# Attention with transposes two slots behind their scores and an exponential that works in place

## The chip, the cores and the metric

The kernel runs on one core of a Trainium2 chip. The metric is the device time of one execution in microseconds (us). Five engines work side by side, each through its own list of instructions and in the order of that list: TensorE (PE) multiplies and transposes, VectorE (DVE), ScalarE (ACT) and GpSimd (POOL) do the elementwise work, and SyncE (SP) hands transfers to the DMA queue. Each waits with semaphores for what the others have to deliver. PE writes its results to PSUM banks; another engine has to copy a bank out before PE may write to it again.

## The reference

```python
scores = scale * np.matmul(q, k.transpose(0, 1, 3, 2))      # 4 batches, 8 heads, 576 x 576
scores = scores + bias.transpose(2, 0, 1)[None]             # bias from a small network over distances
scores = scores - np.max(scores, axis=-1, keepdims=True)
attn = np.exp(scores)
attn = attn / (np.sum(attn, axis=-1, keepdims=True) + 1e-09)
x = np.matmul(attn, v)                                      # then (2304 tokens, 512)
...
x = (g(x @ w_in)) @ w_out                                   # g: hardswish, 2048 wide
x = (sigmoid(x @ w_gate) * (x @ w_val)) @ w_out2            # 1536 wide
```

The change touches the attention alone.

## The kernel before, in words

**Stages.** First the bias of the scores is computed and written to DRAM in 18 transfers, through tiles called `p` (`bias_out`, L548 to L558). Then come attention, the first feed-forward layer (from L601 on) and the second one.

**Units and steps.** Attention runs over 16 units, each a pair of heads of one batch (`NU`). A unit has nine steps. Steps 0 to 7 are the four chunks of 128 query rows for both heads (step s is chunk s//2 of head s%2), each against all 576 keys. Step 8 takes the last 64 rows of both heads together.

**What a step does.** `scores` (L332) multiplies queries and keys on PE into one of two `s` banks (L341; eight matmuls, because queries and keys are split into a high and a low part). VectorE adds the bias, scales, and keeps each row's extreme value in one custom instruction (L345) that writes the tile `u`. `expo` (L359) has ScalarE take the exponential of `u` with the row's extreme as its bias; it writes the tile `p`, and the sums of the rows go to `sums` (L361). The transposes `trans` (L393; L399 on PE, or L407 for step 8) turn the probabilities so that keys lie on partitions; the copies out of the `tr` bank into `ptm` stand in `evac` (L389 on ScalarE, L391 on VectorE). After steps 1, 3, 5 and 8, `trans_rem` (L411, L414) turns the 64 remaining keys into `ptr`. `invert` (L364) takes reciprocals of the sums and spreads them along rows, and `turn_inv` (L374, L378) turns them into `inv`. The products with the values, `av` (L423; L431 for the groups of 128 keys, L434 for the rest), go to the one `av` bank, and `av_out` (L443) multiplies by `inv` on VectorE into the tokens.

**Input.** `load_qk` and `load_v` issue the transfers of a unit's queries, keys and values (L288, L290, L294). `prep` (L303) makes the high and low parts: L309 on ScalarE, L313 and L317 on GpSimd.

**Order.** `slot_of_two(i)` issues the work of steps 2i and 2i+1 in a row: scores and loads, the products that the table `AV` gives to the slot, the exponentials, `invert` of the slot before, `turn_inv` of two slots before, the transposes of the slot before (not ahead of the slot's last score matmul), then `prep`. There are `NSLOT` slots. A scheduler takes these instructions and settles the order of each engine; it may move them past one another where dependences allow. Around it the weight loader of the feed-forward layer is called every six slots (`load.whole`, L158 to L192), `split_x(0)` at slot 72, and the first two projections of the feed-forward layer ("early projections", `begun`) at slots 73 and 74, of which the ones on PE are L601 to L603 and the evictions L607 and L608.

**Buffers.** PSUM has two `s` tiles of two banks, three `tr` banks and one `av` bank. In SBUF `u` has three buffers, `p` three (each holds a chunk of both heads), `vn` two; `spread`, `inv`, `ptm`, `ptr` have one each.

Of the kernel before, what the change touches and what calls it, by code (L numbers as in the profile page):

```python
# [10 lines left out]
F32 = mybir.dt.float32  # L11
F32R = mybir.dt.float32r
I32 = mybir.dt.int32
AF = mybir.ActivationFunctionType
# [4 lines left out]
P = 128  # L19
B, H, S, D = 4, 8, 576, 64  # L20
# [5 lines left out]
NSTEP = 9  # L26
# [69 lines left out]
def block_kernel(ctx: ExitStack, tc: tile.TileContext, q, k, v, mlp, w_in, w_out, w_gate, w_val, w_out2, dist_d,  # L96
                 rows_d, out):
    nc = tc.nc
# [166 lines left out]
    a2 = attn.enter_context(tc.tile_pool(name="a2", bufs=2))  # L265
# [14 lines left out]
    low, sums = [stat[:, i] for i in range(2)], [stat[:, i] for i in range(2, 5)]  # L280
# [44 lines left out]
    NS = NU * NSTEP  # L325
    ptm = apool.tile([P, 2, 4, S], F32, name="ptm")
    ptr = apool.tile([P, S], F32, name="ptr")
    pts, us, avs, last_u, last_s = {}, {}, {}, [None], [None]
# [3 lines left out]
    def scores(t):  # L332
        n, s = seq[t]
        Q, K = Qs[n % 2], Ks[n % 2]
        ps = pp.tile([P, 2, 512], F32, name="s")
        todo = [(s % 2, s // 2)] if s < 8 else [(0, 4), (1, 4)]
        for a in range(2):
            mm = [(h, c, r) for h, c in todo for r in range(2)]
            for i, (h, c, r) in enumerate(mm):
                q0 = (0, S + P)[h] + P * c if c < 4 else (512, S)[h]  # L340
                last_s[0] = nc.tensor.matmul(ps[:, a, 0:HS], Q[:, q0 : q0 + P], K[:, r, h, HS * a : HS * a + HS],  # L341
                                 start=(i == 0), stop=(i == len(mm) - 1))
        u = a2.tile([P, S], F32, name="u", bufs=3)
        bt = bias_t[s // 2][:, s % 2] if s < 8 else bias_m
        last_u[0] = nc.vector.tensor_tensor_reduce(  # L345
            out=halves(u), in0=ps[:, :, 0:HS], in1=halves(bt), op0=ALU.add, op1=ALU.min, scale=-0.125, scalar=3e38,
            accum_out=low[n % 2][:, s : s + 1])
        us[t] = u

    def probs(t):  # L350
        n, s = seq[t]
        if s < 8:
            c, h = divmod(s, 2)
            if h == 0:
                pts[n, c] = a2.tile([P, 2, S], F32, name="p", bufs=3)
            return pts[n, c][:, h]
        return Pm[n % 2][:, 64:]

    def expo(t):  # L359
        n, s = seq[t]  # L360
        nc.scalar.activation(probs(t), us.pop(t), AF.Exp, bias=low[n % 2][:, s : s + 1], scale=-1.0,  # L361
                             accum_out=sums[n % 3][:, s : s + 1])

    def invert(n, c0, c1):  # L364
# [82 lines left out]
    REM = {1: 0, 3: 1, 5: 2, 8: 3}  # L447
    last_v = [None]

    NSLOT = NS // 2 + 4  # L450
    AV = {}
    for n in range(NU):
        i = (NSTEP * n + 5) // 2 + 2
        j = max(i + 2, (NSTEP * n + 8) // 2 + 2)
        for a, first in ((0, i), (1, j)):
            AV[first] = [(n, a, g) for g in range(3)]
            AV[first + 1] = [(n, a, g) for g in range(3, 5)]

    def steps(i):
        return [t for t in (2 * i, 2 * i + 1) if 0 <= t < NS]  # L460

    def slot_of_two(i):

        for t in steps(i):
            scores(t)
            n, s = seq[t]
            p, b = divmod(n, B)
            if s == 0:
                last_v[0] = load_v(n)
            if b == B - 1 and p + 1 < NPAIR and (s % 2 == 1 or s == 8):  # L470
                load_bias(p + 1, s // 2)
        for n, a, g in AV.get(i, ()):
            av(n, a, g)
            if g == 4:
                av_out(n, a)
        for t in steps(i):
            expo(t)
        for t in steps(i - 1):
            n, s = seq[t]
            if s in (5, 8):  # L480
                invert(n, s // 6 * 3, s // 6 * 2 + 3)
        for t in steps(i - 2):
            n, s = seq[t]
            if s in (5, 8):
                turn_inv(n, s // 6 * 3, s // 6 * 2 + 3)
        for t in steps(i - 1):
            n, s = seq[t]
            with tc.issue_after(last_s[0].ins):
                trans(t)
                if s in REM:  # L490
                    trans_rem(n, REM[s])
        for t in steps(i):
            if t in PREP:
                n, h = PREP[t]
                prep(n, h)
            for k, (n, h) in PREP.items():
                if h == 1 and n + 1 < NU and t == k + 3:
                    load_qk(n + 1)
# [6 lines left out]
    with ExitStack():  # L505
# [41 lines left out]

        def bias_out(G, ps):  # L548
            if G % 2 == 0:
                evs[0] = a2.tile([P, 2, S], F32, name="p", bufs=3)  # L550
            ev = evs[0]
            b = corr[:, 1:2] if G % ACT_SKIP == ACT_SKIP - 1 else corr[:, 0:1]
            nc.scalar.activation(halves(ev[:, G % 2]), ps[:, :, 0:HS], AF.Identity, bias=b, scale=rpsi8[:, G : G + 1])
            if G % 2 == 1:
                c, r = divmod(16 * (G - 1), P)
                last_b[0] = nc.sync.dma_start(nbias[c][r : r + 32].rearrange("(g i) h j -> (i h) g j", g=2), ev)
                if r == P - 32 or G == S // 16 - 1:
                    load_bias(0, c)  # L558

        evs, last_b = [None], [None]  # L560
# [175 lines left out]
        for part2, t in todo:  # L736
            for f in range(NH * part2, NH * part2 + NH):
# [9 lines left out]
                if part2 and t in (3, 5) and f % NH == NH - 3:  # L747
                    j = t // 4
# [168 lines left out]
```

## Time and profile before

| | |
|---|---|
| median of three runs | 1172.85 us (1172.06 to 1176.66) |
| profiled execution | 1173.17 us |
| its span, first to last instruction | 1171.4 us |
| mean granted clock of TensorE | 0.998 |
| busy: PE, weight loads, DVE, ACT, POOL | 98%, 87%, 66%, 50%, 35% |
| data moved by DMA | 236.87 MB, 202 GB/s in the mean |
| first scores; end of attention's stage | 60.60 us; about 349 us |

A busy PE has some matmul in flight. The ends of matmuls are modelled in the profile, so that 98% does not say that it runs at its peak. The weight loads (PEld) overlap the matmuls and have their own share. An engine's idle time is put down to the instruction that ended it. Start times count from the beginning of the span.

### The profile page before, as it was taken

How to read it: one execution, taken by the hardware profiler on the slowest of the kernel's cores; microseconds unless marked ns; L12 is line 12 of the kernel's file. 1: busy time of each engine (PE TensorE's matmuls, PEld its weight loads, DVE VectorE, ACT ScalarE, POOL GpSimd, SP SyncE). 2: the span in 40 equal slices, each digit the busy share in tenths (PEclk: the TensorE clock that was granted, in tenths of full speed). 3: DMA queues.
4: the chain of work that ended last, by engine and by line, in shares of the span. 5: the costliest groups of instructions: out<-in, count | busy, mean ns of one | idle time of the engine just before them, and what ended most of it. 6: DMA issues, size and time to landing. Idle time of an engine off the chain costs nothing.

```text
span 1171.4 us, 19580 instructions
## 1 busy us (share of the span) xinstructions
PE 1149.3 (98%) x7086; PEld 1020.6 (87%) x7086; DVE 772.2 (66%) x1484; ACT 590.0 (50%) x1272; POOL 413.9 (35%) x342
## 2 busy tenths in 40 slices
PE   8999999999999899999999999999999999999998
PEld 3467777777779899999999999999898998998997
DVE  8967787878868777447376576576357646543443
ACT  7978878787855455444454544443223222221211
POOL 0055445545305333233155534363223313311211
PEclk9999999999999999999999999999999999999999
DMA  6653635335213555339565658888768858757532
GB/s 205 252 150 96 209 92 183 100 103 165 95 43 120 189 206 193 131 120 320 216 243 215 250 183 333 340 319 326 273 232 279 319 172 321 280 179 263 189 109 72
DMA packets 80737, 236.87 MB, mean 202 GB/s; under 512 B 9088, under 2 KB 11904, under 8 KB 80640
## 3 DMA queue, kind: packets, MB, share of 16 engines
q1 hardware_dynamic: 80640, 235.62, 57.9%
q8 instruction: 56, 0.92, 0.3%
q14 instruction: 41, 0.34, 0.1%
HBM read 154.45 MB, written 81.13 MB: 201 GB/s over the span
## 4 chain that ended last, share of the span: by engine, by line
PE 78%; DVE 10%; ACT 4%; issue 4%; DMA 3%; POOL 1%; SPq 0%; DVEq 0%; POOLq 0%; ACTq 0%
PE o L664 12%; PE h L798 11%; PE o L798 11%; PE s L341 6%; PE o L853 6%; PE h L853 6%; PE av L431 5%; PE tr L399 4%; PE h L602 4%; PE h L601 4%; PE h L603 4%; PE s L575 2%; DVE z L185 2%; PE av L434 1%; DMA third<-in_part_dram 1%
## 5 line engine op out<-in xcount | busy, mean ns | idle before, releaser
L664 PE MATMUL o<-gh,slot 128*128 128x384 f32 x768 | 196.9, 337 | 6.4 <-ACT take L389 4.2
L664 PEld LDWEIGHTS o<-gh,slot 128*128 128x128 f32 x768 | 139.0, 189 | 8.7 <-ACT take L389 4.5
L664 PE MATMUL o<-gl,slot 128*128 128x384 f32 x384 | 129.4, 337 | 0.8 <-DVE gl L650 0.8
L361 ACT ACTIVATE p<-u,stat 128x576 f32<-128x576 f32 x128 | 98.7, 773 | 31.8 <-DVE stat L345 31.2
L341 PE MATMUL s<-k,q 128*128 128x288 f32 x640 | 112.2, 310 | 2.1 <-POOL k L317 1.0
L192 POOL TENSOR_TENSOR hl<-corners,hl 128x512 fp32r<-128x512 f32 x42 | 58.2, 1394 | 157.0 <-ACT hl L191 135.6
L650 DVE TENSOR_TENSOR gl<-g,gh 128x384 fp32r<-128x384 f32 x94 | 73.3, 779 | 60.2 <-ACT gh L649 60.0
L345 DVE CUSTOM_DVE_ANT_0 u<-s,bias 128x576 f32<-128x576 f32 x128 | 93.6, 753 | 26.7 <-PE s L341 26.2
L608 DVE SCALAR_TENSOR_TENSOR g<-g,h 128x384 f32<-128x384 f32 x94 | 51.7, 550 | 73.6 <-ACT g L607 73.4
L834 POOL TENSOR_TENSOR gp<-s,gp 128x384 fp32r<-128x384 f32 x36 | 39.7, 1115 | 160.0 <-PE h L798 104.3
L341 PEld LDWEIGHTS s<-k,q 128*128 128x128 f32 x640 | 89.1, 189 | 5.4 <-POOL k L313 1.9
L431 PE MATMUL av<-ptm,vn 128*64 128x288 f32 x512 | 78.2, 419 | 1.2 <-DVE x L443 0.7
L798 PE MATMUL o<-x,slot 128*128 128x384 f32 x432 | 77.8, 335 | 0.0
L798 PE MATMUL h<-x,slot 128*128 128x384 f32 x432 | 77.8, 335 | 0.0
L798 PEld LDWEIGHTS h<-x,slot 128*128 128x128 f32 x432 | 75.2, 188 | 0.7
L798 PEld LDWEIGHTS o<-x,slot 128*128 128x128 f32 x432 | 75.1, 188 | 0.0
L399 PE MATMUL tr<-ident,p 128*128 128x128 f32 x512 | 72.2, 275 | 2.2 <-ACT inv L389 1.5
L664 PEld LDWEIGHTS o<-gl,slot 128*128 128x128 f32 x384 | 72.5, 189 | 1.8 <-DVE gl L650 1.8
L649 ACT CAST gh<-g 128x384 fp32r<-128x384 f32 x94 | 48.1, 512 | 51.5 <-DVE g L608 51.0
L607 ACT ACTIVATE g<-h,half 128x384 f32<-128x384 f32 x94 | 54.2, 576 | 37.6 <-PE h L603 37.5
L317 POOL TENSOR_TENSOR q<-early,q 64x640 fp32r<-64x640 f32 (+1 forms) x30 | 44.2, 1485 | 74.3 <-ACT q L309 72.9
L834 POOL TENSOR_TENSOR x<-s,x 128x384 fp32r<-128x384 f32 x36 | 41.1, 1150 | 82.2 <-ACT x L833 48.1
(157 smaller groups left out, 2714.9 us busy)
## 6 DMA issues: line engine op xcount, KB each, us to landing
w<-hl SPq DMA_DIRECT2D x67, 512.0 KB, 3.4
slot<-w SPq DMA_DIRECT2D x67, 512.0 KB, 5.8
raw<-in_part_dram SPq DMA_DIRECT2D x50, 512.0 KB, 3.7
x<-xc SPq DMA_DIRECT2D x56, 384.0 KB, 6.2
sum<-sum SPq DMA_DIRECT2D x72, 256.0 KB, 3.1
early<-xc SPq DMA_DIRECT2D x28, 384.0 KB, 6.4
nbias<-p SPq DMA_DIRECT2D x18, 576.0 KB, 3.1
early<-in_part_dram SPq DMA_DIRECT2D x32, 288.0 KB, 4.4
```

The costliest lines, as they stand in the source:

```text
L192: eng.tensor_tensor(out=slot[:, 1], in0=z, in1=slot[:, 0].bitcast(F32), op=ALU.subtract)
L341: last_s[0] = nc.tensor.matmul(ps[:, a, 0:HS], Q[:, q0 : q0 + P], K[:, r, h, HS * a : HS * a + HS], start=(i == 0), stop=(i == len(mm) - 1))
L345: last_u[0] = nc.vector.tensor_tensor_reduce(out=halves(u), in0=ps[:, :, 0:HS], in1=halves(bt), op0=ALU.add, op1=ALU.min, scale=-0.125, sc ...
L361: nc.scalar.activation(probs(t), us.pop(t), AF.Exp, bias=low[n % 2][:, s : s + 1], scale=-1.0, accum_out=sums[n % 3][:, s : s + 1])
L399: nc.tensor.transpose(ps[:, kc], pts[n, c][:, h, 64 * h + P * kc : 64 * h + P * kc + P], ident)
L431: nc.tensor.matmul(ps[64 * h : 64 * h + 64, 0:HS], vt[:, 4 * h + g], ptm[:, h, g, cols], start=(g == 0), stop=False)
L607: nc.scalar.activation(g, ph, AF.Relu, bias=half, scale=1.0 / 6.0)
L650: last_g[0] = nc.vector.tensor_tensor(out=gl, in0=g, in1=gh.bitcast(F32), op=ALU.subtract)
L664: nc.tensor.matmul(os[c][:, 0:TW], sl[:, r, P * c : P * c + P], x, start=(first and r == 0 and x is gh), stop=(last and x is gl))
L798: nc.tensor.matmul(ps[b], sl[:, r, o : o + P], x[:, c, s], start=(k < 4 and i == 0), stop=(i == len(mm) - 1), skip_group_check=True)
L834: nc.gpsimd.tensor_tensor(out=G[:, i, 1], in0=s, in1=G[:, i, 0].bitcast(F32), op=ALU.subtract)
L853: nc.tensor.matmul(os[i], x[:, P * i : P * i + P], slots[(base + 14 + e) % NALL][:, r], start=first, stop=last)
```

## The change

It does four things. The biased scores go into the tile that will hold the probabilities, `probs(t)`, and no longer into `u`; the tile `u` is dropped. The exponential reads and writes that same tile. `p` has four buffers where it had three. And the transposes, with the products and the number of slots behind them, follow their scores by two slots where they followed by one.

```diff
@@ scores
-        u = a2.tile([P, S], F32, name="u", bufs=3)
+        u = probs(t)
@@ probs
-            if h == 0:
-                pts[n, c] = a2.tile([P, 2, S], F32, name="p", bufs=3)
+            if (n, c) not in pts:
+                pts[n, c] = a2.tile([P, 2, S], F32, name="p", bufs=4)
@@ expo
-        nc.scalar.activation(probs(t), us.pop(t), AF.Exp, bias=low[n % 2][:, s : s + 1], scale=-1.0,
+        u = us.pop(t)
+        nc.scalar.activation(u, u, AF.Exp, bias=low[n % 2][:, s : s + 1], scale=-1.0,
                              accum_out=sums[n % 3][:, s : s + 1])
@@
-    NSLOT = NS // 2 + 4
+    NSLOT = NS // 2 + 5
...
-        i = (NSTEP * n + 5) // 2 + 2
-        j = max(i + 2, (NSTEP * n + 8) // 2 + 2)
+        i = (NSTEP * n + 5) // 2 + 3
+        j = max(i + 2, (NSTEP * n + 8) // 2 + 3)
@@ slot_of_two
-        for t in steps(i - 1):
+        for t in steps(i - 2):
             n, s = seq[t]
             with tc.issue_after(last_s[0].ins):
                 trans(t)
@@ bias_out
-                evs[0] = a2.tile([P, 2, S], F32, name="p", bufs=3)
+                evs[0] = a2.tile([P, 2, S], F32, name="p", bufs=4)
```

Lines behind L351 have a number one higher in the changed kernel. The scheduler's order moves at many places; three follow.

The first is on PE at the first scores of unit 1. `s_980` and `s_1016` are that unit's score tiles before (`s_956` and `s_987` now), `k1` and `q1` its keys and queries, `tr_*` the transpose banks, `p_*` the probabilities of steps of unit 0, `av_*` its products and `spread` its reciprocal sums. Before:

```order
L399 MATMUL tr_957<-ident_234,p_909 128x128 x4
L414 MATMUL tr_963<-ident_234,p_909 128x128
L341 MATMUL s_969<-k0_230,q0_228 128x288 x4
L431 MATMUL av_989<-ptm_239,vn_847 64x288
L378 MATMUL tr_999<-ident_234,spread_236 128x128 x3
L431 MATMUL av_989<-ptm_239,vn_847 64x288 x4
L341 MATMUL s_980<-k1_231,q1_229 128x288
L431 MATMUL av_989<-ptm_239,vn_847 64x288 x2
L341 MATMUL s_1016<-k1_231,q1_229 128x288
L341 MATMUL s_980<-k1_231,q1_229 128x288 x3
L399 MATMUL tr_1004<-ident_234,p_945 128x128 x4
```

and with the change:

```order
L400 MATMUL tr_934<-ident_234,p_866 128x128 x4
L415 MATMUL tr_940<-ident_234,p_866 128x128
L341 MATMUL s_946<-k0_230,q0_228 128x288 x4
L379 MATMUL tr_967<-ident_234,spread_236 128x128 x3
L341 MATMUL s_956<-k1_231,q1_229 128x288
L341 MATMUL s_987<-k1_231,q1_229 128x288
L341 MATMUL s_956<-k1_231,q1_229 128x288 x3
L400 MATMUL tr_972<-ident_234,p_881 128x128 x4
L400 MATMUL tr_978<-ident_234,p_881 128x128 x4
L415 MATMUL tr_984<-ident_234,p_881 128x128
```

The products of unit 0 (`av_989`), and the transposes of two more steps with one remainder, stood ahead of or among unit 1's first score matmuls; now they come behind them.

The second is on PE at the start of a unit (unit 2 here), around the transposes of `spread`, which stand in a `tr` bank like all others. Before:

```order
L341 MATMUL s_1205<-k0_230,q0_228 128x288 x4
L431 MATMUL av_1212<-ptm_239,vn_987 64x288 x6
L378 MATMUL tr_1226<-ident_234,spread_236 128x128 x3
L399 MATMUL tr_1231<-ident_234,p_1138 128x128 x4
L407 MATMUL tr_1237<-ident_234,pm1_233 128x64 x4
L341 MATMUL s_1260<-k0_230,q0_228 128x288 x4
L407 MATMUL tr_1243<-ident_234,pm1_233 128x64 x4
```

and with the change:

```order
L341 MATMUL s_1172<-k0_230,q0_228 128x288 x4
L379 MATMUL tr_1184<-ident_234,spread_236 128x128 x3
L400 MATMUL tr_1189<-ident_234,p_1040 128x128 x4
L415 MATMUL tr_1195<-ident_234,p_1040 128x128
L400 MATMUL tr_1198<-ident_234,p_1094 128x128 x4
L341 MATMUL s_1208<-k0_230,q0_228 128x288 x4
```

The three `tr` banks are taken in turn. Before, eight transposes in two other banks and a half of a step's scores stand between `tr_1226` and the next use of its bank, `tr_1243`; now five transposes stand between `tr_1184` and the next use of its bank, `tr_1198`, with no scores between. This sequence (three of `spread`, four, one, four) occurs in 5 of the 16 units.

The third is on VectorE at the end of attention. `z_4301` (`z_4153` now) is the first early projection's result, `z_4322` (`z_4174`) the weight loader's tile with its four steps L175 to L187, `x2_65` the output step's tokens. Before:

```order
L391 COPY inv_237<-tr_4295 128x128
L391 COPY inv_237<-tr_4295 64x64
L608 SCALAR_TENSOR_TENSOR z_4301<-z_4301,s_4302 128x384
L175 TENSOR_SCALAR z_4322<-z_4322 128x512
L183 TENSOR_SCALAR z_4322<-z_4322 128x512
L185 SCALAR_TENSOR_TENSOR z_4322<-raw_4198,z_4322 128x512
L187 SCALAR_TENSOR_TENSOR z_4322<-raw_4198,z_4322 128x512
L443 TENSOR_TENSOR x2_65<-av_4325,inv_237 128x288
L650 TENSOR_TENSOR gl_4409<-z_4301,gh_4408 128x384
```

and with the change:

```order
L392 COPY ptm_239<-tr_4140 128x4x64
L392 COPY ptr_240<-tr_4146 64x64
L609 SCALAR_TENSOR_TENSOR z_4153<-z_4153,s_4154 128x384
L175 TENSOR_SCALAR z_4174<-z_4174 128x512
L444 TENSOR_TENSOR x2_65<-av_4115,inv_237 128x288
L183 TENSOR_SCALAR z_4174<-z_4174 128x512
L185 SCALAR_TENSOR_TENSOR z_4174<-raw_4036,z_4174 128x512
L187 SCALAR_TENSOR_TENSOR z_4174<-raw_4036,z_4174 128x512
L444 TENSOR_TENSOR x2_65<-av_4197,inv_237 128x288
L651 TENSOR_TENSOR gl_4265<-z_4153,gh_4264 128x384
```

One output step now stands between the loader's first and second step. On PE at that place, behind the first early projection, stood six instructions of L431, the second early projection, then two of L431 and the unit's closing product L434; now two of L431 and a closing product come first, then the second projection, then eight of L431 and the last closing product. From there on each engine has the same instructions in the same order.

## Rows read from the trace of the kernel before

**Rows 1.** The page's first part: busy us (share of the span) xinstructions of each engine.

```profile
PE 1149.3 (98%) x7086; PEld 1020.6 (87%) x7086; DVE 772.2 (66%) x1484; ACT 590.0 (50%) x1272; POOL 413.9 (35%) x342
```

**Rows 2.** Windows by stage: us, busy (xcount) of each engine, PEclk, DMA share, GB/s.

```profile
60.60:78.00 17.40, 14.61 (x99) 11.22 (x98) 11.53 (x28) 13.68 (x33) 7.93 (x7) 1.00 0.59 173
78.00:348.50 270.50, 267.37 (x1960) 203.33 (x1959) 212.94 (x547) 212.72 (x555) 126.08 (x95) 1.00 0.40 118
```

**Rows 3.** PE's waits, 78 to 349 us: total us, times, longest.

```profile
PE tr L399 <- ACT inv L389: 1.5, 3, 0.5
PE tr L399 <- DVE ptm L391: 0.7, 3, 0.2
PE av L431 <- DVE x L443: 0.7, 3, 0.2
PE tr L414 <- ACT ptm L389: 0.3, 1, 0.3
```

**Rows 4.** Timeline around unit 1's first scores: start us, us, engine, line, operation [idle before].

```profile
66.58 0.46 SPq L300 DMA_DIRECT2D bias_m<-nbias  x1
...
67.55 0.76 DVE L345 CUSTOM_DVE_ANT_0 u<-s,bias 128x576 f32<-128x576 f32 x1
...
72.92 2.25 POOL L313 TENSOR_TENSOR k<-early,one 128x576 fp32r<-128x576 f32 x2 [1.37 <-DMA early<-in_part_dram]
...
74.12 0.40 PE L341 MATMUL s<-k,q 128*128 128x288 f32 x1 [0.77 <-POOL k L313]
...
75.22 0.40 PE L341 MATMUL s<-k,q 128*128 128x288 f32 x1
...
76.58 0.66 PE L341 MATMUL s<-k,q 128*128 128x288 f32 x3 [0.96 <-POOL k L317]
```

**Rows 5.** Chain of waits: start us, us, engine, line, xcount; attention's stage and after.

```profile
82.85 1.61 PE av L431 x12
...
320.91 0.87 PE tr L399 x8
...
331.31 0.68 PE av L434 x2
...
343.75 0.59 ACT z L607
...
392.51 3.90 PE o L664 x12
...
402.66 2.08 PE o L664 x12
```

**Rows 6.** Timeline of one `spread` bank and its copy, near 337 us.

```profile
337.40 0.55 PE L378 MATMUL tr<-ident,spread 128*128 128x128 f32 x3
...
337.99 0.48 ACT L389 COPY inv<-tr 128x384 f32<-128x384 f32 x1 [0.47 <-PE tr L378]
```

**Rows 7.** Instructions by line, 60 to 349 us: the exponential and the reading of its sum.

```profile
L361 ACT ACTIVATE p<-u,stat 128x576 f32<-128x576 f32 x128 | 98.7, 773 | 31.8 <-DVE stat L345 31.2
...
L361 ACT ACTIVATION_READ_ACCUMULATOR p<-u,stat 128x1 f32 x128 | 24.2, 189 | 0.0
```

**Rows 8.** Timeline of VectorE at the last output step.

```profile
348.98 0.46 DVE L443 TENSOR_TENSOR x<-av,inv 128x288 f32<-128x288 f32 x1 [0.72 <-PE av L434]
```

**Rows 9.** Timeline of SyncE's queue, 157 to 167 us.

```profile
158.48 0.33 SPq L294 DMA_DIRECT2D vn<-in_part_dram  x1
...
165.74 1.11 SPq L290 DMA_DIRECT2D early<-in_part_dram  x2
```

**Rows 10.** Window just behind the wait near 392 us.

```profile
392.50:396.40 3.90, 3.89 (x13) 3.90 (x14) 3.59 (x8) 2.00 (x5) 0.93 (x1) 0.56 0.91 333
```

## The prediction

> **What bounds the kernel now.** I read four views, in this order. The page's busy shares come first [rows 1]: TensorE (PE) has a matmul in flight for 98% of the span, the other engines for 35 to 66%. The windows [rows 2] divide that by stage. The stage that the change touches runs from the first scores (60.6 us) to the last attention matmul (about 348.5). In it the reader should see two different stretches: from 78.00 to 348.50 PE is busy for 267.37 of 270.50 us, so 3.1 us are idle in all; from 60.60 to 78.00 it is busy for 14.61 of 17.40. The list of PE's waits [rows 3] tells what the few long waits of the first stretch are for: the copies that empty PSUM banks (`inv` and `ptm`, released by ScalarE or VectorE) and the output step that frees the one `av` bank. No row has a transpose waiting for an exponential, and that dependence is the one which the change loosens. The timeline of the second stretch [rows 4] shows what PE does wait for there: the keys of unit 1. They are prepared on GpSimd behind a DMA, and PE gets the high part of head 0 at 74.12 (after 0.77 us of waiting), that of head 1 at 75.22, and the low part at 76.58 (after 0.96).
>
> So attention is bound by PE's own stream, with one appointment that does not depend on PE: 76.58.
>
> **The change, part by part.**
>
> *Transposes and products one slot later, at the start.* TensorE takes its instructions in order, and the order (first piece in the section on the change) shows what stands ahead of unit 1's first scores. Before: 24 step transposes, 3 remainder transposes, and 7 products of `av` interleaved up to the third score matmul. Now: 16, 2 and none. The missing 8 + 1 transposes cost 0.87 us for 8, which is 0.11 each, or 0.98 together. The missing 7 products have two records each, and 12 records take 1.61 us, so 14 take 1.88 [rows 5]. That is 2.9 us of work with which PE filled the wait for the keys and which it now has still to do at 76.58. The keys do not come sooner: their DMA, the casts on ScalarE and the subtractions on GpSimd stand in the same order as before up to there. PE does run ahead, but only into that wait. From 77 us on it has next to no idle time in which to catch up [rows 2], so the whole 2.9 us stay. Bounds: 2.0 if some of the work finds cover between the three arrivals, 3.5 if the ScalarE casts come later and the keys with them. I take **+2.9**.
>
> *Waits on PSUM banks.* The transposes share three banks before and after, `s` has two and `av` one; the change gives none. Below, all 3.1 us of idle time could vanish. Above, the order of the new kernel has a place that was not there: at the start of a unit (second piece) the bank of the `spread` transposes is wanted again after only 5 further transposes, in 5 of the 16 units. The nearest rows [rows 6]: the copy of that bank starts 0.59 us after the first `spread` transpose and lasts 0.48, so the bank is free 1.07 us after it; PE wants it after 3 + 5 transposes, 0.87 us. That is 0.2 us each if ScalarE is free, and 0.96 more (0.773 for an exponential, 0.189 for reading its sum [rows 7]) if one is in front: 1.0 to 5.8 us in all. I take the low end, because the scheduler gave this place a gap of nearly the right size, and let half a microsecond of the old waits go: **+0.5**, between -3.1 and +5.8.
>
> *The end of attention.* One slot more is drained, but with the same instructions, so PE's sum does not change. After attention every engine's order is the same as before. What changes is what follows the first early projection: before 6 products, the second projection, 2 products and the last one; now 2 products and a last one, the projection, 8 products and a last one. By the same rows that is 1.2 us more PE work behind it, so it ends 1.2 us earlier relative to the end of attention. It matters because the chain of waits goes from that projection's eviction at 343.75 through the weight loader to 392.51 [rows 5], where PE stands idle for it. VectorE gives some of it back: the output step (0.46 us [rows 8]) now stands between the loader's first two steps (third piece), and the last output step has to wait for the later end. I put that at 0.8 of the 1.2: **-0.4**, between -1.2 and +0.5.
>
> *Costs put at nothing.* The exponential in place reads and writes as many elements as before (0.773 us); only its addresses change. VectorE's score step writes `p` where it wrote `u`, at equal length. It must now find the `p` tile free: in steady state a buffer comes back after 8 or 9 steps, while its last transposes are done one slot (two steps) before that. The first time round it must wait for the bias pass's DMAs; the last has landed when the queue issues the next load at 66.58, and step 6, which is the first to write that buffer, ran at 67.55 [rows 4]. If the step came earlier, the wait would fall into the time before 74.12, where PE stands anyway. SyncE's queue: the load of `vn` waits for `av` of two units before, now one slot later (270.50 us for some 70 slots [rows 2], 3.8 us), and the next unit's keys stand behind it; in the trace that key load was issued 7.3 us after `vn` [rows 9], so 3.5 us of cover remain. The bias loads of the next pair move ahead of a `vn` and a `raw` load; both have several steps to spare.
>
> *Sum.* The profiled execution took 1173.17 us. 1173.17 + 2.9 + 0.5 - 0.4 = 1176.2. Its time stands 0.3 above the median of the runs, 1172.85, so I predict **1175.9**. A measurement of this kernel can tell about 0.5% from no change, that is 5.9 us, so this is "no difference", on the slow side.
>
> **Rivals.**
>
> *The clock falls at the start as well.* PE now would do next to nothing from about 70 to 76.58. The trace has one such place: after 4.2 us idle at 392.51 the granted clock averages 0.56 of full over the next 3.9 us [rows 10], the lower of its two levels (1.2 GHz) for most of it, and 12 matmuls take 3.90 us instead of 2.08 [rows 5]. That would add 1.8: 1177.7. For it: the gap is longer than that one. Against it: three arrivals and three `spread` transposes break it up, and before, with 0.77 and 0.96 us waits close together, nothing fell. The Trainium skill ("TensorE: Matmul & The Clock Gate", Part 1) says that PE's clock has two levels and goes to the lower when the engine idles; by that rule this change costs the 1.8 us, and the row at 392.51 agrees with the rule.
>
> *Slower: the new bank wait with an exponential in front.* The place is the `spread` bank above, five times, at 1.16 us each: 1176.2 - 0.5 + 5.8 = 1181.5, or 1181.2 against the median. It decides if ScalarE has an exponential queued ahead of the `inv` copy in most of these units. For it: ScalarE is busy for 212.72 of 270.50 us [rows 2], and three of the old waits are for a copy of `inv` on ScalarE [rows 3]. Against it: in the new order the copy stands ahead of the next exponentials there.
>
> *The old waits go.* If more distance lets the copies come in time, the 3.1 us go: 1173.17 + 2.9 - 0.4 - 3.1 = 1172.6, or 1172.3 against the median. For it: they lie at fixed places in the loader's slots. Against it: none of them waits for an exponential.
>
> *Faster: hidden slack in PE.* Weight loads are busy for only 203.33 of 270.50 us [rows 2], 67.2 us less. If a fifth of that were short waits inside the matmuls' modelled lengths, and distance removed them, 13.4 us would go: 1162. Against it: spacings of 0.11 and 0.13 us recur unit after unit [rows 5], which waits would not do, and the counts of PE's changes from one kind of work to another hardly differ in the two orders (456 and 458). The Trainium skill ("Perfetto Trace Analysis", section Identifying the Most-Contended Engine) says to judge PE's headroom by weight loads and not by matmul occupancy; by it a quarter of the stage would be free, and the even spacings here speak against that.
>
> That the change does not do what it says is excluded by the order: every step's transposes stand two slots behind.
>
> **How the numbers follow.** Forecast 0.46 (some 1173.5 to 1178), clock 0.24 (1176 to 1180), slower by bank waits 0.14 (1179 to 1184), old waits go 0.10 (1171.5 to 1173.5), faster 0.06. The range 1171.5 to 1181.0 leaves out the faster case and half of the bank case, and little more. Slower by over 0.5% (above 1178.7): 0.09 of the clock case, 0.12 of the bank case, 0.03 of the forecast: 0.24. Faster by over 0.5% (below 1167.0): 0.06. The rest, 0.70, within.
>
> **What would show it.** Right: the timeline shows PE idle ahead of unit 1's first scores for about 3 us in all more than before, with the keys still arriving near 74.1 and 76.6; the last attention matmul comes about 3 us later than 348.5; the stage from 78 us on has about as much idle time as now; the wait ahead of the first output products near 392 is about as long, and shifted by 2 to 3 us. Wrong: the keys arriving earlier, work other than these products and transposes filling the gap, or idle time of PE after 78 us above 6 us or near nothing. A granted clock below 1 between 70 and 82 us would show the clock rival.

## The result, and where the time went

The changed kernel takes 1189.95 us in the median of five runs (1188.62 to 1194.68), the kernel before 1173.32 in runs beside it: ratio 1.0146, 95% interval 1.0133 to 1.0160. It is 16.6 us slower. The forecast was 1175.9 with a range to 1181.0, so the time lies outside of it, on the side that was given 0.24. The profiled execution took 1189.09 us, with a span of 1187.3. Four executions of the kernels below took 2250 to 6360 us, and no median or ratio counts them.

The first part of the page (busy us, share of the span, xinstructions), after the change:

```profile
PE 1158.4 (98%) x7086; PEld 1025.8 (86%) x7086; DVE 769.6 (65%) x1484; ACT 591.2 (50%) x1272; POOL 413.7 (35%) x342
```

Against [rows 1] the span grew by 15.9 us. PE's share is still 98%, but its busy time grew by 9.1 us with the same 7086 instructions, and the other 6.8 are idle. Two things have happened to PE: it waits more, and its own work has become longer. The prediction had allowed for the first alone.

The windows by stage after the change (us, busy time with xcount of PE, PEld, DVE, ACT and POOL, granted clock, DMA share, GB/s), the first two as in [rows 2], the third across their border:

```profile
60.60:78.00 17.40, 11.48 (x67) 9.19 (x66) 8.80 (x25) 12.49 (x31) 8.16 (x7) 0.86 0.53 157
78.00:348.50 270.50, 263.18 (x1875) 196.32 (x1874) 203.64 (x528) 205.92 (x535) 123.95 (x94) 1.00 0.43 118
70.00:82.00 12.00, 7.43 (x36) 5.74 (x36) 3.70 (x11) 7.06 (x19) 8.60 (x7) 0.72 0.41 101
```

Before, PE was busy for 14.61 us of the first window at a granted clock of 1.00, and issued 1960 matmul records in the second; now it is busy for 11.48 at 0.86, and issues 1875. Its idle time in the second window is 7.3 us, where it was 3.1. I also set PE's instructions of the two traces side by side by the work done, with each kind counted at its usual spacing (a score matmul 0.13 us, a transpose 0.11). The new kernel's first scores start 0.8 us earlier. At the work that the old one does at 87 us it is 4.2 behind; at 317 us, 17.6; at 361 us, 16.5. So the start cost 4.2 us, the units after it 13.4, and the end of attention gave 1.1 back; these are estimates, good to some tenths. From the first output products on the distance hardly changes: they start at 408.88 instead of 392.51, 16.4 later.

PE's waits by what released them (total us, times, longest us) show the same two stretches. From 60 to 82 us, after:

```profile
PE s L341 <- POOL k L313: 3.0, 2, 2.5
PE tr L379 <- ACT spread L373: 1.4, 1, 1.4
PE s L341 <- POOL k L317: 0.8, 1, 0.8
```

and from 82 to 366 us, the last attention matmul:

```profile
PE tr L415 <- DVE ptm L392: 2.6, 4, 0.8
PE tr L408 <- ACT inv L390: 2.3, 2, 1.5
PE s L341 <- DVE stat L345: 2.1, 6, 0.4
```

The copies of [rows 3] are still there, ahead of other transposes and for longer (up to 1.5 us), and the score step is new. Four mechanisms stand behind these numbers; each has its rows here, and its runs in the next section.

**The start.** The timeline of PE ahead of unit 1's first scores, and two pieces of the chain of waits (start us, us, what):

```profile
70.83 0.55 PE L379 MATMUL tr<-ident,spread 128*128 128x128 f32 x3 [1.37 <-ACT spread L373]
...
73.87 0.61 PE L341 MATMUL s<-k,q 128*128 128x288 f32 x1 [2.50 <-POOL k L313]
...
74.98 0.61 PE L341 MATMUL s<-k,q 128*128 128x288 f32 x1 [0.49 <-POOL k L313]
...
76.34 1.09 PE L341 MATMUL s<-k,q 128*128 128x288 f32 x3 [0.75 <-POOL k L317]
```

```profile
77.42 1.71 PE tr L400 x8
...
408.88 4.21 PE o L665 x12
```

The keys come at the old times [rows 4]; PE waits longer for them, and then eight transposes take 1.71 us where eight took 0.87 [rows 5]. The granted clock was at the lower level (1.2 GHz) from 73.4 to 80 us.

**Broken pairs.** A product of `av` uses 64 of the array's 128 columns (`128*64` in its row), one half for each head, and has two records. The two heads' products run at the same time if they are neighbours in PE's order: their records start 6 to 7 ns apart in the trace, and the next two 0.24 us later. In the new order some are not neighbours, and each of their records then takes 0.24 to 0.34 us by itself. The timeline of PE near 99 us:

```profile
98.57 0.70 PE L432 MATMUL av<-ptm,vn 128*64 128x288 f32 x2
99.20 0.44 PE L379 MATMUL tr<-ident,spread 128*128 128x128 f32 x2
99.44 0.40 PE L341 MATMUL s<-k,q 128*128 128x288 f32 x1
99.77 1.67 PE L432 MATMUL av<-ptm,vn 128*64 128x288 f32 x10
```

The first two records are a product that stands alone, and so are the last two of the ten, which take 1.67 us; all twelve together took 1.61 [rows 5]. The lines of the products, before and after:

```profile
L431 PE MATMUL av<-ptm,vn 128*64 128x288 f32 x512 | 78.2, 419 | 1.2 <-DVE x L443 0.7 <-DVE ptm L391 0.5
```

```profile
L432 PE MATMUL av<-ptm,vn 128*64 128x288 f32 x512 | 82.9, 419 | 0.0
```

The same 512 records of the same mean length, 419 ns, cover 4.7 us more: they overlap less. No wait is named, and the busy share hides it.

**A blocked addition.** VectorE adds 1e-9 to the row sums (L368, at most 6 elements a row; L367 before). The timeline near 113 us:

```profile
113.02 1.41 POOL L317 TENSOR_TENSOR k<-early,k 128x576 fp32r<-128x576 f32 x1
...
113.32 1.14 DVE L368 TENSOR_SCALAR stat<-stat 128x3 f32<-128x3 f32 x1
...
114.49 0.18 DVE L369 RECIPROCAL stat<-stat 128x3 f32<-128x3 f32 x1
...
114.58 0.66 DVE L392 COPY ptm<-tr 128x512 f32<-128x512 f32 x1
...
115.30 0.33 PE L415 MATMUL tr<-ident,p 128*128 128x128 f32 x1 [0.80 <-DVE ptm L392]
```

The addition takes 1.14 us, until GpSimd's subtraction ends at 114.43; elsewhere it takes 0.16. Behind it on VectorE stands the copy that PE waits for. It took over 0.9 us in 11 of 32 cases now, in 8 before, and seven of the 11 are followed by one of PE's waits of 0.3 to 0.8 us, 3.7 us in all.

**Late raw weights.** SyncE's queue loads `vn` and behind it the weight loader's raw weights; ScalarE, the queue of the loader's first step (L174), then waits. After the change:

```profile
130.27 0.54 SPq L294 DMA_DIRECT2D vn<-in_part_dram  x1
...
130.87 0.42 SPq L158 DMA_DIRECT2D raw<-in_part_dram  x1
...
138.56 0.66 ACT L174 ACTIVATE z<-raw 128x512 f32<-128x512 f32 x1 [2.03 <-DMA raw<-in_part_dram]
...
139.24 0.21 ACT L390 COPY inv<-tr 64x64 f32<-64x64 f32 x1
...
139.50 0.33 PEld L408 LDWEIGHTS tr<-ident,pm 64*128 64x128 f32 x4 [1.09 <-ACT inv L390]
```

and the same place in the kernel before:

```profile
122.91 0.43 SPq L158 DMA_DIRECT2D raw<-in_part_dram  x1
...
131.04 0.69 ACT L174 ACTIVATE z<-raw 128x512 f32<-128x512 f32 x1 [0.19 <-DMA raw<-in_part_dram]
```

Before, the step already met its data to 0.2 us. Now the transfer is issued 8 us later, behind the pair's bias loads, and the step 7.5 later, with the copy of `inv` and PE behind it.

### The profile page after: what moved, and what is told of

It is laid out like the page before. It is cut to its first block, busy times and chain, and to the rows that moved or that the text cites. A ratio compares the mean times of both kernels' runs of the same rounds, so it can differ in the third digit from the quotient of the medians.

```text
span 1187.3 us, 19539 instructions
## 1 busy us (share of the span) xinstructions
PE 1158.4 (98%) x7086; PEld 1025.8 (86%) x7086; DVE 769.6 (65%) x1484; ACT 591.2 (50%) x1272; POOL 413.7 (35%) x342
## 4 chain that ended last, share of the span: by engine, by line
PE 78%; DVE 8%; DMA 4%; ACT 4%; issue 3%; POOL 1%; SPq 0%; DVEq 0%; ACTq 0%; POOLq 0%
PE o L665 12%; PE h L799 11%; PE o L799 11%; PE o L854 6%; PE h L854 6%; PE s L341 6%; PE av L432 5%; PE h L603 4%; PE h L602 4%; PE h L604 4%; PE tr L400 4%; DMA raw<-in_part_dram 3%; PE s L576 2%; PE av L435 2%; DVE z L185 1%
## 5 line engine op out<-in xcount | busy, mean ns | idle before, releaser
L341 PE MATMUL s<-k,q 128*128 128x288 f32 x640 | 114.9, 313 | 6.5 <-POOL k L313 3.0
L362 ACT ACTIVATE p<-p,stat 128x576 f32<-128x576 f32 x128 | 98.5, 772 | 30.7 <-DVE stat L345 30.1
L345 DVE CUSTOM_DVE_ANT_0 p<-s,bias 128x576 f32<-128x576 f32 x128 | 93.3, 752 | 18.2 <-PE s L341 16.9
L341 PEld LDWEIGHTS s<-k,q 128*128 128x128 f32 x640 | 90.6, 191 | 12.9 <-DVE stat L345 6.0
L432 PE MATMUL av<-ptm,vn 128*64 128x288 f32 x512 | 82.9, 419 | 0.0
L400 PEld LDWEIGHTS tr<-ident,p 128*128 128x128 f32 x512 | 58.7, 142 | 15.9 <-issue 10.1
```

The source lines that it names most:

```text
L345: last_u[0] = nc.vector.tensor_tensor_reduce(out=halves(u), in0=ps[:, :, 0:HS], in1=halves(bt), op0=ALU.add, op1=ALU.min, scale=-0.125, sc ...
L362: nc.scalar.activation(u, u, AF.Exp, bias=low[n % 2][:, s : s + 1], scale=-1.0, accum_out=sums[n % 3][:, s : s + 1])
L400: nc.tensor.transpose(ps[:, kc], pts[n, c][:, h, 64 * h + P * kc : 64 * h + P * kc + P], ident)
L432: nc.tensor.matmul(ps[64 * h : 64 * h + 64, 0:HS], vt[:, 4 * h + g], ptm[:, h, g, cols], start=(g == 0), stop=False)
```

## The experiments

A ratio goes by the runs of a kernel against those of the kernel before on the same chip; gains and losses below are differences of ratios times 1173 us, each uncertain by 2 to 3 us. The changed kernel's ratio is 1.0146.

**In place alone.** The kernel before with the change's buffers, at one slot:

```diff
-        u = a2.tile([P, S], F32, name="u", bufs=3)
+        u = probs(t)
...
-        nc.scalar.activation(probs(t), us.pop(t), AF.Exp, ...
+        nc.scalar.activation(u, u, AF.Exp, ...
```

> The kernel before with only the buffers changed: scores written into p, exponential in place, p with four buffers, transposes one slot behind as before. Every engine's order is that of the kernel before. Theory (all of the 16.6 us comes from the later transposes and what the order made of them): 1172 to 1175 us, no difference. Rival (the in-place exponential, or p held longer by the score step, costs time by itself): 1178 us or more, with VectorE's score steps waiting for the transposes that free p.

Measured: 1173.21 us, ratio to before 0.9993 (0.9985 to 1.0002). The buffers and the exponential in place cost nothing; the whole loss comes with the second slot.

**The addition, two ways.** First its elements were put at every second place:

```diff
-    stat = apool.tile([P, 5, NSTEP], F32, name="stat")
+    stat = apool.tile([P, 5, NSTEP, 2], F32, name="stat")
```

> The changed kernel with the row sums and extremes stored at every second element, so that VectorE's tiny addition to the sums (L368) has no even run of neighbours; the order on every engine is that of the changed kernel, instruction for instruction. Theory (the addition stands still until GpSimd's running subtraction ends, 1.0 to 1.4 us in 12 of 32 cases, and seven of these are followed by PE waits of 0.64 to 0.96 us, 5.2 us in all): the addition lasts 0.2 us everywhere, the seven waits go, 1184 to 1187 us. Rival (the addition waits for GpSimd whatever its stride, or PE's waits there have another cause): 1188.5 to 1191 us.

> The kernel before with the same spacing of sums and extremes; order unchanged on every engine. In its trace the addition lasted 1.0 to 1.3 us in 7 of 32 cases, and PE's waits for ptm copies behind it are 0.37 to 0.40 us three times. Theory: 1171 to 1173 us, some 1 us less at most. Rival (the step matters as much here as in the changed kernel): 1168 to 1170 us.

Measured: 1191.37 us (ratio 1.0144, 1.0125 to 1.0163), and 1173.68 for the kernel before (0.9996, 0.9987 to 1.0005). Spacing changes nothing: 11 of 32 additions still took over 0.6 us. A miss, and the rival's second half stayed open, so next the instruction itself was changed:

```diff
-        nc.vector.tensor_scalar(out=r, in0=r, scalar1=1e-9, scalar2=None, op0=ALU.add)
+        nc.vector.reciprocal(junk[:, 0 : min(2 * c1, NSTEP) - 2 * c0], r)
```

> The changed kernel with the addition of 1e-9 to the row sums left out and a reciprocal into an unused tile in its place; that is the only difference in any engine's order. Reciprocals lasted 0.17 to 0.20 us even where GpSimd worked from before their start until after their end (11 times), the addition up to 1.4. Theory (seven PE waits, 5.2 us, come from the blocked addition): 1184 to 1186 us, and the waits of PE for ptm copies near 115, 153, 228 and 301 us and for the score step near 170, 245 and 318 us are gone. Rival (these waits have other causes): 1188.5 to 1191 us.

Measured: 1186.33 us, ratio 1.0108 (1.0093 to 1.0122), a gain of 4.5 us (3.6 by the medians). VectorE's line in its trace, where 32 additions took 17.2 us:

```profile
L369 DVE RECIPROCAL junk<-stat 128x6 f32<-128x6 f32 (+1 forms) x32 | 5.7, 178 | 2.8 <-ACT pm L363 1.7 <-ACT p L363 0.8
```

PE's waits for VectorE's `ptm` copies are gone (2.6 us before), and those for the score step fell from 2.1 to 0.7. The one for `inv` grew from 2.3 to 3.5, and behind one of its parts (1.52 us) the granted clock was at 0.50 from 285.7 to 292.3 us: part of the gain moved to the next wait.

**Whole pairs.** The second head's product is traced first and the first head's ordered behind it:

```diff
-            for h in range(2):
-                nc.tensor.matmul(...)
+            first = one(1)
+            with tc.issue_after(first.ins):
+                one(0)
```

> The changed kernel with the second head's product traced first and the first head's ordered behind it, so that no product of one head stands alone in PE's order (before 4 lone ones in 2 broken pairs, changed 20 in 10, here none). Theory (two heads' products run at the same time only as neighbours, and a broken pair costs 0.3 to 0.5 us): 3 to 5 us less than the changed kernel, 1185 to 1187 us. Rival (the first product now waits for the second head's copy, and the gain is given back): 1188.5 to 1191 us.

Measured: 1188.30 us, ratio 1.0110 (1.0092 to 1.0128), a gain of 4.2 us, although the median is above the expected range. The products cover 76.8 us, 6.1 less, and the wait for `inv` rose from 2.3 to 4.2. Behind its two parts (1.60 and 2.55 us) the granted clock was at 0.50 from 139.4 to 142.7 and from 214.5 to 217.7 us, which it was not in the changed kernel: some of what whole pairs save goes there. With the addition replaced as well:

> The changed kernel with no broken pair of products and with the blocked addition replaced (the addition of 1e-9 is left out). Alone the first took away 1.6 us and the second 3.6. Theory (the two add up, and the 7 us that whole pairs save between PE's instructions show once the waits that took their place go): 1181 to 1185 us. Rival (whichever wait is removed, PE runs into the next one): 1186 to 1188 us.

Measured: 1185.01 us, ratio 1.0102 (1.0086 to 1.0118). That is 5.2 us of gain, at the upper end of the theory, and less than the 8.7 that the two alone would add up to, though not clear of their uncertainty. PE still waits for ScalarE's copies of `inv` (3.5 us) and `ptr` (2.5), and ScalarE for raw weights eight times, 9.4 us in all.

**The start covered.** Unit 0 follows at one slot, units 1 to 15 at two:

```diff
+    def turned(i):
+        early = [t for t in steps(i - 1) if t < NEAR1]        # NEAR1 = 10
+        return [t for t in steps(i - 2) if t >= NEAR1] + early
...
+        lag = 2 if n == 0 else 3
```

> The changed kernel with unit 0's transposes and products one slot behind, as before the change, and those of all other units two slots behind. Theory (5.8 of the 16.6 us are lost ahead of unit 1's first scores, where PE has nothing to do for 5 us and its clock is then granted at half until 80 us): the granted clock stays at 1.00 between 70 and 82 us, PE's waits there fall to those of the kernel before, 1183 to 1186 us. Rival (the gap only shows a loss that comes back later, as waits for banks in the units that follow): 1188 to 1191 us.

Measured: 1188.54 us (1184.61 to 1192.09), ratio 1.0125 (1.0102 to 1.0147), a gain of 2.5 us. In its trace the start is mended, with a clock of 1.00 and 8.94 us busy from 70 to 82 us, and by work done it runs 0.1 us behind the kernel before at 93 us, where the changed one is 4.3 behind. By the figures of the last section 4.2 us were lost at the start, and not the 5.8 of the expectation. So the theory holds for the start, but the time lies in the rival's range, and the gain is no larger than its uncertainty. Part of it is lost again further on, as these windows, and ScalarE ahead of them, show:

```profile
209.47 0.66 ACT L174 ACTIVATE z<-raw 128x512 f32<-128x512 f32 x1 [3.29 <-DMA raw<-in_part_dram]
```

```profile
208.00:211.00 3.00, 0.87 (x8) 0.57 (x7) 0.76 (x2) 1.48 (x4) 2.75 (x2) 1.00 0.03 12
211.00:214.00 3.00, 3.00 (x11) 1.73 (x11) 2.91 (x9) 1.50 (x5) 0.00 (x0) 0.52 0.58 128
```

Here ScalarE waited 3.29 us for raw weights, PE 2.13 for the copy behind it, and the granted clock fell to 0.52. In the changed kernel's trace the wait at that place was 1.48 and the clock stayed at 1.00. So a wait of this size may cost its own length or more, which fits the spread of these runs.

**The raw weights, two ways.** A third buffer for `vn`, or the loader called at `i % EVERY == 1` instead of 0:

> The changed kernel with three buffers for the values, so that SyncE's queue no longer stands at their load until the products of two units before are done. Theory (the loader's raw weights come too late behind that load, ScalarE and VectorE stand at the loader's first steps three times, and PE's waits of 0.92 and 1.54 us near 139 and 214 us follow): these waits go, 1186 to 1188 us. Rival (the late weights cost nothing by themselves): 1188.5 to 1191 us.

> The changed kernel with the weight loader called one slot later, so that its steps on ScalarE and VectorE move along with its delayed transfers. Theory (the same late weights): ScalarE's waits for raw weights go, 1186 to 1188 us. Rival (they cost nothing by themselves): 1188.5 to 1191 us. Against the gain: one more pair of products is broken in four units (11 split groups where the changed kernel has 7), up to 2 us.

Measured: 1201.64 us (ratio 1.0234, 1.0218 to 1.0249) and 1188.34 (1.0122, 1.0108 to 1.0136). The first is a miss. The raw weights come sooner, but the order moves at many places on every engine, ScalarE waits for them longer than in the changed kernel (11.1 us against 6.7 up to 380 us), and the loader's steps on VectorE fall into GpSimd's subtractions. Its line and the changed kernel's:

```profile
L187 DVE SCALAR_TENSOR_TENSOR z<-raw,z 128x512 int32<-128x512 int32 x12 | 12.8, 1068 | 0.2
```

```profile
L187 DVE SCALAR_TENSOR_TENSOR z<-raw,z 128x512 int32<-128x512 int32 x12 | 8.2, 686 | 0.2
```

PE then waits 11.3 us for `ptm` copies, and from the longest two of these waits on (2.3 and 2.0 us) the granted clock is at half for nearly 7 us each. In the second run, a gain of 2.8 us, the wait for `inv` is gone, and the wait for `ptm` copies grew from 2.6 to 4.6.

**All four, and all but one.** Whole pairs, the replaced addition, the later loader and the covered start in one kernel:

> The changed kernel with all four parts put right: unit 0 one slot behind, no broken pair, no blocked addition (1e-9 left out), the loader one slot later; units 1 to 15 still have their transposes two slots behind. Theory (these four make up nearly all of the 16.6 us, and distance itself costs nothing): 1174 to 1179 us. Rival (the distance itself makes PE meet VectorE and ScalarE out of step, and a wait that is removed comes back elsewhere): 1181 to 1187 us.

Measured: 1175.67 us, ratio 1.0017 (1.0007 to 1.0027), with 15 units still two slots behind. The four edits take away 15.1 us (1.0146 less 1.0017), and 2.0 are left. That distance itself costs nothing is not shown by this: whole pairs and the replaced addition help the kernel before a little as well (0.9989, further below), and against that one 3.3 us are left, uncertain by 1.8. Then each was put back:

> As the kernel with all four parts put right (1175.7 us), but unit 0 two slots behind again. Theory (the start costs 4 to 6 us by itself): 1179.5 to 1181.5 us, with the granted clock near half from 74 to 80 us. Rival (the start's loss is hidden by other waits, as the small gain of the run with unit 0 alone, 1188.5 us, would have it): 1176 to 1178 us.

> As the kernel with all four, but products of the two heads traced as in the changed kernel; PE's order has 11 groups split in 1 and 5 (21 lone products). Theory (0.3 to 0.5 us for a broken pair, and a slot's rhythm that it upsets): 1179 to 1182 us. Rival (only waits matter): 1175 to 1177 us.

> As the kernel with all four, but with the addition of 1e-9 back in its place; no other instruction differs on any engine. Theory (VectorE's blocked addition makes PE wait wherever transposes stand two slots behind): 1178 to 1181 us. Rival (with the pairs whole and the loader later, the addition falls where it delays nothing, as in the kernel before): 1175 to 1177 us.

> As the kernel with all four, but the loader in its old slots. Theory (late raw weights hold up ScalarE and VectorE, and PE behind them): 1178 to 1182 us. Rival (the raw weights cost PE nothing): 1175 to 1177 us.

| part | taken from the change alone | gain | put back into all four: median us, ratio (interval) | loss |
|---|---|---|---|---|
| start | 1.0125 | 2.5 us | 1178.26, 1.0040 (1.0024 to 1.0055) | 2.7 us |
| broken pairs | 1.0110 | 4.2 us | 1179.08, 1.0052 (1.0036 to 1.0068) | 4.1 us |
| blocked addition | 1.0108 | 4.5 us | 1179.84, 1.0054 (1.0037 to 1.0071) | 4.3 us |
| early loader | 1.0122 | 2.8 us | 1180.38, 1.0063 (1.0043 to 1.0084) | 5.4 us |
| sum | | 14.0 us | | 16.5 us |

Within their intervals the two columns agree with one another and their sums with the 15.1. Three of the gains are clear of their uncertainty (that of the start is not), and all four losses, so each of the four carries a share, and none of them explains the loss by itself. How large each share is remains rough. Only the addition can be put back without moving any other instruction; with the other three the scheduler changes the order elsewhere too. And the start is not wholly mended in all four: in its trace the granted clock is 0.79 from 74 to 82 us, where it is 0.57 with the start put back and 1.00 with the broken pairs, so the 2.7 us of the start (below the 4 to 6 that were expected) may be too low. What a broken pair does shows most plainly in the traces. The window of attention, and the line of the products, with the pairs broken:

```profile
82.00:345.00 263.00, 262.76 (x1875) 195.34 (x1873) 193.02 (x528) 205.31 (x537) 121.08 (x92) 1.00 0.42 119
```

```profile
L433 PE MATMUL av<-ptm,vn 128*64 128x288 f32 x512 | 87.3, 420 | 0.0
```

and with all four put right:

```profile
82.00:345.00 263.00, 259.31 (x1905) 195.57 (x1905) 195.50 (x534) 209.76 (x545) 121.45 (x92) 1.00 0.42 120
```

```profile
L433 PE MATMUL av<-ptm,vn 128*64 128x288 f32 x512 | 76.3, 419 | 0.0
```

PE has no idle time left with the broken pairs, 0.24 us of 263, and does less: 1875 records against 1905. In PE's order none of the pairs is broken in all four, 2 before, 10 after the change, 16 here, and the products cover 76.3, 78.2, 82.9 and 87.3 us: which is 0.66 and 0.69 us for each of the 10 and the 16. The starts say the same: the four records of a broken pair take 1.2 us, those of a whole one 0.56. The time of the kernel moved by less, 4.1 us for the 16, since 3.5 us of PE's idle time went at the same time.

**Before, improved.** The pairs and the addition in the kernel before:

> The kernel before with its two broken pairs kept whole and the blocked addition replaced (1e-9 left out). Theory (two pairs at 0.35 to 0.5 us, and three waits of 0.4 us behind the blocked addition): 1171 to 1172.5 us, faster than both kernels by a hair. Rival (PE's waits there have other causes): 1173 to 1174 us.

Measured: 1171.97 us, ratio 0.9989 (0.9978 to 1.0001). If it is faster, the runs can't tell.

**The keys sooner.** Unit 1's keys ahead of the last bias loads on SyncE's queue:

```diff
+                if G == S // 16 - 1:
+                    with tc.issue_after(last_b[0].ins):
+                        load_qk(1)
+                    with tc.issue_after(last_k[0].ins):
+                        load_bias(0, c)
```

> The changed kernel with the transfers of unit 1's keys issued ahead of the last two bias loads on SyncE's queue instead of behind them; nearly nothing else in any order moves. Theory (the start's loss is the wait for unit 1's keys, which the later transposes left uncovered, and the half clock behind it): the keys reach PE some 4 us sooner, no granted clock below 0.9 between 70 and 82 us, 1184 to 1187 us. Rival (the two bias loads, now behind the keys, become the wait): 1188 to 1191 us.

> The kernel before with the same two transfers moved. PE's waits for the keys there are 0.77 and 0.96 us and one short one. Theory: 1.5 to 2.5 us less than the kernel before. Rival (the bias loads are late, or the time comes back at the next wait): within 1 us of it.

> The kernel before with unit 1's keys loaded ahead of the last bias loads and its two broken pairs kept whole; everything is computed. Theory: the two gains add to 2 to 3.5 us less than the kernel before. Rival: the same time as with the keys alone.

Measured: 1188.75 us (1.0121, 1.0103 to 1.0138), 1176.36 (1.0020, 1.0012 to 1.0028), and 1176.00 (1.0014, 1.0005 to 1.0023). Theory missed in all three; the first is 2.9 us below the changed kernel by its ratio, at the edge of what can be told. The timeline of the second:

```profile
71.39 2.25 POOL L315 TENSOR_TENSOR k<-early,one 128x576 fp32r<-128x576 f32 x2
...
72.59 0.19 PEld L343 LDWEIGHTS s<-k,q 128*128 128x128 f32 x1 [1.78 <-POOL k L315]
72.59 0.40 PE L343 MATMUL s<-k,q 128*128 128x288 f32 x1 [1.27 <-POOL k L315]
...
75.05 1.09 PE L343 MATMUL s<-k,q 128*128 128x288 f32 x3 [1.73 <-POOL k L319]
```

and the window behind it:

```profile
74.00:82.00 8.00, 6.95 (x29) 4.78 (x29) 1.93 (x6) 2.32 (x7) 2.36 (x2) 0.57 0.29 74
```

The keys land 3 us sooner, but GpSimd is busy with the queries' subtraction until 71.3, so PE gets them only 1.5 us sooner, at 72.59 and 75.05. The scheduler put the scores forward accordingly, with PE's other work behind them; the waits became 1.27 and 1.73 us where they were 0.77 and 0.96 [rows 4], and the mean clock of the 8 us from 74 on fell from 1.00 to 0.57. The appointment at the start bears on the clock even in the kernel before.

No version that was run beats the kernel before beyond its interval.

## Why the prediction was wrong, step by step

**What bounds the kernel.** Right in that PE's stream sets the time and that unit 1's keys are an appointment. They are not the only one: the raw weights are another, as below. The reading of [rows 2], that PE had 3.1 us of idle time, said nothing of how much PE's stream can grow. In the sum the units after the start stood with +0.5 us; they cost 13.4. The sign that was set for being wrong came too: PE's idle time after 78 us is 7.3 us, above 6.

**The start, +2.9: the term was about right, and the clock came on top.** The keys did come at the old times, and the missing products and transposes left PE waiting. By work done it cost 4.2 us. The rival on the clock, at 0.24, was what happened here, and its 1.8 us are about right: from 76.5 to 80 us PE's spacings are 0.10 us longer each, 1.8 in all. With the keys 0.24 us earlier, 2.9 and 1.8 make 4.5. The wait for `spread` (1.37 us) adds nothing, since PE would have waited for the keys behind it. The Trainium skill's rule on the clock ("TensorE: Matmul & The Clock Gate", Part 1) spoke for that rival, and the eight transposes at 1.71 us agree.

**Waits on banks, +0.5: the place was right, the cause incomplete.** In five units the transposes that take the bank of `spread` again start 0.19 us late, against 0.2 predicted. But the sum took this place for the only new one. The waits that came stand on VectorE and ScalarE, behind an instruction that neither of these engines decides: the addition that GpSimd blocks, and the loader's step behind a transfer. I had looked at what the orders of PE hold, and not at what each delayed copy stands behind.

**"With the same instructions, so PE's sum does not change": the step that failed most.** The sentence stands at the end of attention, and the whole sum rests on it: that PE's own work keeps its length was given no other reason. PE's busy time grew by 9.1 us, some of it at half clock, and the products' cover by 4.7 us. I counted how often PE changes from one kind of work to another (456 and 458), and did not ask which changes are new. The order had them: single products of L432, split from their neighbours.

**Costs put at nothing.** The exponential in place and the buffers: right, as the first run shows. SyncE's queue: right for the keys, wrong for "a `raw` load; both have several steps to spare". The row of 131.04 in the trace of before says that the loader's step had 0.2 us of waiting there already, and nothing to spare.

**The end, -0.4.** It gave about 1.1 by work done, nearly the whole of the bound of 1.2; why VectorE took less back than the 0.8 expected was not looked into.

**The slower rival** had the right sign and a wrong price and place, 1181 us with a bank behind an exponential. **The rival that PE's headroom could make it faster** fell. What would have told them apart beforehand was in the profile: the records of L431 overlap more than others (512 at 0.419 us are 214.5 us in 78.2, 2.7 times; 640 of L341 at 0.310 are 198 in 112.2, 1.8 times), so their order matters.

## What to carry to other kernels

When a change leaves every instruction as it is and moves only their order, look at what runs beside what: neighbours on one engine that run at the same time, instructions that two engines can't run at the same time, and steps that meet their transfer with nothing to spare. Search the trace of before for the last two, since they are already there as rows with an odd length or a short wait. And when several causes are found, take them all away in one kernel and put them back one at a time: that shows whether they make up the whole.

## What was not expected of the hardware

- A VectorE addition of three elements a row takes 0.16 us alone and up to 1.42 beside a GpSimd subtraction, and ends within 0.03 us of it; spacing its elements apart changes nothing, while reciprocals lasted 0.17 to 0.18 us inside GpSimd's work. The Trainium skill ("SBUF — State Buffer", section SBUF: two separate sides) tells of a port pair that VectorE's faster modes and GpSimd hold by turns for a whole instruction; the ends agree with it. That spacing is no way out fits the Trainium skill's "VectorE: DVE Perf Modes" (section What auto-detection actually checks), which for 32-bit elements names no stride among the conditions.
- Two heads' products ran side by side only as neighbours; each broken pair lengthens the time that the products cover by 0.66 to 0.69 us and shows in no wait.
- Waits of PE of 2.13 us, or of 1.27 and 1.73 us with little between, were followed by 3 to 7 us at half of the clock; 0.77 and 0.96 us were not. The length of the wait alone does not tell: 1.48 us near 214 us in the changed kernel was not followed by a fall, and 1.48 us near 138 us in the run with whole pairs and the replaced addition was.
